# A new written order for the last two stages of a gated attention and feed-forward kernel

## The chip, the cores and the metric

The kernel runs on one core of a Trainium2 chip. The metric is the device time of one execution in microseconds (us), lower is better. A core has TensorE (PE in the rows; its weight loads are PEld), VectorE (DVE), ScalarE (ACT), GpSimd (POOL) and SyncE (SP), which here only issues DMAs. Each engine works through its own instructions in the order in which the program wrote them, and waits at an instruction until what it reads is ready and the buffer that it writes is free.

## The reference

The result is a gated mix of linear attention and a feed-forward layer over the same input, in float32: 2048 tokens, width 640, 32 heads of 20 features, hidden width 1728.

```python
g = _sigmoid((x * gate_w).sum(-1, keepdims=True))
qkv = ...                                     # x @ wqkv, by head
pq = jnp.einsum("bhsd,hdf->bhsf", q, w_phi)
phi_q = jnp.concatenate([_softmax(pq, axis=-1), _softmax(-pq, axis=-1)], axis=-1)
...                                           # phi_k the same from k
kv = jnp.einsum("bhsf,bhsd->bhfd", phi_k, v)
z  = jnp.einsum("bhsf->bhf", phi_k)
num = jnp.einsum("bhqf,bhfd->bhqd", phi_q, kv)
den = jnp.einsum("bhqf,bhf->bhq", phi_q, z)[..., None] + 1e-6
a = (num / den) @ wo                          # heads joined
b = silu(x @ w1) @ w2
out = g * a + (1 - g) * b
```

## The kernel before, in words

Nearly every product is made of three float32r matmuls: both factors are split into a high part (a cast on ACT) and a low part (a subtraction on DVE or POOL). The kernel first sums keys and values over all tokens, then runs the feed-forward layer in pairs of weight rows over two halves of the tokens, and ends with two stages whose order is written out by hand in two strings, `TAIL` and `FIN`. A loop pops the words of a string one by one and calls what stands under each word; `inorder` ties every instruction to the one before it on the same engine, so the string is the order of all five engines at once, SP's DMA issues included.

`TAIL` finishes the feed-forward layer and starts the queries: `fm`/`fs` join the query weights with the feature map (`pwq`), `qp12` to `qp15` are the query products of the last four token tiles (128 tokens each), `hm`/`hp` two last hidden rows, `im`/`ia` ten output products (`o`) and their additions, `km`/`kp` eleven small transposes that turn the key-value sums (`pkvt`).

`FIN` takes the other twelve token tiles and writes the result. A word has a letter and numbers:

- `q3p`: query product of the fourth of these tiles, 30 matmuls of 320 columns. Then on DVE `m`, `s0`, `s1` (extremes and differences), on ACT `e` (exponential), on POOL `z` and `M` (two 128x1280 products), on DVE `S`, `Z`, `P`, `i`, `k` (sums and factors), on ACT `g` (two copies and two DMAs that send the features to memory, `q_out`).
- `t05`, `f05`: transposes of features on PE for token blocks 0, 1 and 7 (256 tokens each) and their copy on ACT. The other blocks come back transposed by DMA (`j`).
- `n04`: product of features with key-value sums for block 0, head group 4 (`pn`, into PSUM); `h02` casts the pair of groups 4 and up into the high part of `oT` (ACT L1769), `l02` subtracts the low part (DVE L1774).
- `z0m`, `z0h`, `z0l`, `z0s`, `z0d`: the leftover columns of block 0. They are multiplied, split, stored to memory (`r_store`, L1798) and loaded into other partitions of `oT` (`r_place`, L1801, called the placing DMA below).
- `w02a`, `w02b`: the two halves of one output product of pass 0 (blocks 0 and 1), 15 matmuls `pa<-oT,wo` (L1836). Pass 1 is blocks 2 and 3, pass 2 blocks 4 and 5, passes 3 and 4 blocks 6 and 7. `y` loads the feed-forward part, `c` gates it (POOL), `d` adds it (DVE L1860), `o` stores the result.
- `x5l`, `x5s`: load and split of input columns for later query products.

A placing DMA writes partitions that the casts of the same block have written over, so it comes after all `h` and `l` of its block, and no `w` of a pass starts before both placing DMAs of its blocks have landed:

```python
def r_place(u):
    nc.sync.dma_start(
        o_cols(u)[KD : P - KD].rearrange("r c s w -> r (c s) w").bitcast(F32),
        r_d[u].rearrange("(r c) s w -> r (c s) w", c=NG),
    )
```

PSUM tiles of the last stage come from four banks named `single` and two pairs for query products, and a product waits until its bank has been read.

Of the kernel before, what the change touches and what calls it, by code (L numbers as in the profile page):

```python
# [73 lines left out]
Y43l v14 Y41h Y42l Y41l e14 xf r14 G43l m14 l14  # L74
"""
TAIL = """
fl1 xl0 hm012 hp012 fm1 fl2 fm2 ol4 fl5 fl4 fs1 fs2 fm4 fl3 fs4 wa fm0 fm5 fs0 fs5 fm3 W fs3 qp12
q012 q112 qp13 q013 qe12 os4 qn12 wb hm013 q113 qe13 xl2 qs13 xs2 hm113 hp013 qp14 ol2 q114 q014
hm112 qs12 qn13 qN13 xl1 os2 xs1 im0 qc13 ia0 qe14 hp113 qn14 qs14 im1 qc12 qP13 qi13 ol1 os1 ol3
qN12 ol0 km kp qN14 os0 qp15 q015 q115 qw13 hp112 ia1 is0 im2 ia2 qP12 is1 xs0 qi12 is2 qc14 qP14  # L80
qm13 os3 qw12 qm12 qe15 im3 ia3 im4 qn15 ia4 im5 qi14 qw14 qm14 is3 is4 qN15 ia5 ig5 im6 ia6 is5
qs15 ig6 im7 qc15 ia7 ig7 qP15 qi15 qw15 qm15 im8 ia8 im9 ia9 ig9 is7 ig8 is6
"""
PASS = """
h0a wh ka h1a h1b h0b us0 wl uh0 xh1 us1 uh1 ul0 h2a h2b us2 h3a ul1 xh3 uh2 h3b xh0 kb xh4 xl3 xh2
# [58 lines left out]
NSEV = (4, 5)  # L144
TPOSE = (0, 1, 7)
FIN = """
q0p t11 q0m q0s0 x10l t01 x4s x10s t00 t05 q1p x3s t12 f01 x14l t03 x14s q0s1 q0e q0z q0S f11 t15
f05 f00 q1m t13 q1s0 f12 x7l f15 z1m z0m n00 f03 z0h q1s1 y03 x5l z1h z1l x6l n01 t02 z0l q0Z t14
f13 t04 q1e q1z y01 f02 t10 x9l q0P z1s f14 n02 q0i q0k f10 n03 z0s h00 n10 n11 f04 q0M x8l x5s n12
n14 l00 n13 h10 q1S x7s q2p q1Z n04 h01 h12 q1P h11 q1i q0g q1k q1M x9s l11 h02 l10 l12 l01 l02 z0d  # L150
q1g x8s q2m z1d q2s0 q3p q2s1 q2e q3m q3s0 q3s1 q2S x12l q2z w00a w00b q3e w02a q2Z w02b q2P q2i q2k
q3S q3z j20 q3Z j21 x6s q3P j22 q4p x13l q3i q3k y02 d02 q2M q2g q5p w01a z2m q4m x11l q3M q4s0 x17l
n20 o02 q4s1 q5m q3g y00 d00 o00 x11s q4e q4z q5s0 y04 q5s1 n22 w01b z2h z2l n23 z2s n24 n21 w04a
q5e h20 h22 q4S j30 d01 q4Z q4P q4i q5z j32 q4k l20 h21 l21 w04b q4M q7p q5Z l22 n30 j31 n31 d04
x13s q5S q4g z3m z3h x15l q5P q5i q5k z3l q7m q5M q7s1 z3s z2d n34 n32 h32 h30 y14 x15s l32 o01 n33
x12s h31 q6p w03a q5g l30 l31 z3d q7s0 q6m w03b q6s1 q6s0 q7e q7S x16l q6e w14a q7z w10a q6z o04 j41
q7Z q7P q7i w10b q8p q7k q7M q6S w14b q7g q6Z q6P q6i q6k q6M q9p x17s q8m y11 q8s1 d14 q6g y10 q8s0
q8e j42 d10 q8z n44 d03 q9m j40 n42 z4m z4h z4l o14 q9s1 n40 n41 h40 n43 h42 h41 o10 w12a w12b o03
y12 w11a l40 q9s0 q8S w11b x16s q11p j50 j52 j51 q8Z q8P q8i q8k q9e q9z n54 d12 l42 z5m q9Z q9S z4s
q8M q8g n52 n53 z5h y23 d11 q9P q9i q9k n50 n51 q10p z5l y20 h50 w13a z5s h51 o11 l41 z4d w13b h52  # L160
o12 l50 l51 l52 z5d q11m gl q9M w20a w20b q11s1 y22 y13 q11s0 q10m w23a q9g q10s0 q11e q11z q11S j60
q10s1 q10e q10S w23b j62 w22a w22b j61 q10z d20 q11Z o20 q11P d23 w24a n60 n61 q11i q11k z6m q10Z
z6h d22 o22 n62 y24 n63 q10P h60 h61 n64 w24b w21a q10i q10k q10M q11M t73 d13 h62 z6l t71 l62 t72
f73 f71 t70 t74 f72 o23 z6s y21 t75 l60 w21b y30 c30 n72 l61 z6d d24 d21 n73 f75 z7m f70 n70 o13 f74
n74 z7h z7l n71 h70 o24 h71 w32a y34 c34 h72 l72 o21 w34a w34b w30a w30b l71 l70 z7s z7d w32b y42
y32 c42 d34 w40a w42a w42b o34 w40b w44a d30 o30 w44b y40 y44 c32 d32 o32 d42 o42 c40 d40 c44 o40
d44 o44
"""
ORDERS = (HEAD, O1, O2, O3, O4, O5, O6, O7, O8, O9, O10)
KEPT = (0, 2)  # L170
# [1813 lines left out]
```

## Time and profile before

| | |
|---|---|
| median of 3 runs | 700.91 us (700.59 to 701.91) |
| profiled execution, its own time | 701.84 us |
| span of its trace | 700.1 us |
| busy: PE, PEld, DVE, ACT, POOL | 99%, 84%, 66%, 45%, 58% |
| chain that ended last: PE, DMA, DVE, ACT | 95%, 2%, 1%, 1% |

The span runs from the first to the last instruction; 1.74 us of the execution lie outside it. In the trace `TAIL` begins at 478.3 us with its first product on PE, and `FIN` at 540.4 us. Times in the rows are counted from the start of the span.

### The profile page before, as it was taken

What the parts mean: (1) busy time and instruction counts of PE and PEld (TensorE: products, weight loads), DVE (VectorE), ACT (ScalarE), POOL (GpSimd) and SP (SyncE); (2) the same over time, 40 slices, a digit from 0 to 9 for tenths busy, and PEclk for the clock granted to TensorE, in tenths of its full rate; (3) what the DMA queues carried; (4) which work ended last, traced back from release to release, by engine and by line L of the source; (5) the groups of instructions that cost most, each with busy time, mean ns of one, the idle gap of its engine ahead of it and who ended that gap; (6) DMA issues with size and microseconds to landing.
All of it is one profiled execution on the core that took longest, in us unless ns stands there. A gap on an engine that the chain in (4) does not pass through costs nothing.

```text
span 700.1 us, 11997 instructions
## 1 busy us (share of the span) xinstructions
PE 691.8 (99%) x4530; PEld 586.8 (84%) x4530; DVE 464.6 (66%) x773; ACT 311.9 (45%) x556; POOL 407.7 (58%) x313
## 2 busy tenths in 40 slices
PE   9999999999999999999999999999999989999998
PEld 7888888888888888888888888788988878888878
DVE  4687978887434465677845556567695788878832
ACT  5344555446554433334455233425561755544230
POOL 2376876595672554574495555840499876665332
PEclk9999999999999999999999999999999999999999
DMA  8447888877584565489386444628013357998944
GB/s 308 144 171 277 323 292 301 284 275 240 172 284 157 204 217 173 155 303 340 115 303 218 138 156 126 202 82 265 25 62 130 122 148 216 227 244 210 215 142 133
DMA packets 88919, 141.75 MB, mean 202 GB/s; under 512 B 38498, under 2 KB 52086, under 8 KB 88862
## 3 DMA queue, kind: packets, MB, share of 16 engines
q1 hardware_dynamic: 83422, 133.77, 59.6%
q10 hardware_dynamic: 5440, 7.21, 2.9%
q8 instruction: 36, 0.59, 0.4%
q14 instruction: 21, 0.17, 0.1%
HBM read 88.61 MB, written 45.14 MB: 191 GB/s over the span
## 4 chain that ended last, share of the span: by engine, by line
PE 95%; DMA 2%; DVE 1%; ACT 1%; SPq 0%; issue 0%; DVEq 0%; ACTq 0%
PE kvp L622 18%; PE o L1240 12%; PE a L1110 10%; PE pa L1836 10%; PE o L1199 9%; PE pq L598 9%; PE o_m L1262 3%; PE ph L688 3%; PE b L1110 3%; PE c L1110 3%; PE d L1110 3%; PE pn L1758 2%; PE hp L707 2%; PE kvt L609 2%; DMA oT<-r_d 1%; PE kvp L493 1%
## 5 line engine op out<-in xcount | busy, mean ns | idle before, releaser
L1230 DVE TENSOR_TENSOR acc<-acc,o 128x512 f32<-128x512 f32 x118 | 77.3, 682 | 42.3 <-PE o L1240 35.0
L622 PE MATMUL kvp<-wh,xa 128*128 128x480 f32 (+2 forms) x420 | 90.3, 358 | 0.0
L622 PEld LDWEIGHTS kvp<-wh,xa 128*128 128x128 f32 x420 | 72.8, 188 | 10.0
L1836 PE MATMUL pa<-oT,wo 128*128 128x512 f32 (+1 forms) x375 | 72.3, 350 | 2.7 <-DMA oT<-r_d 2.7
L1836 PEld LDWEIGHTS pa<-oT,wo 128*128 128x128 f32 x375 | 59.4, 188 | 13.9 <-ACT eq L1337 2.4
L1199 PE MATMUL o<-u,w 128*128 128x512 f32 x280 | 65.5, 390 | 0.0
L1199 PEld LDWEIGHTS o<-u,w 128*128 128x128 f32 x280 | 52.4, 188 | 11.0
L1126 POOL TENSOR_TENSOR u<-v,u 128x512 fp32r<-128x512 f32 x18 | 23.3, 1296 | 65.3 <-ACT u L1125 65.3
L1354 POOL TENSOR_TENSOR ez<-eq,zbc 128x1280 f32<-128x1280 f32 x16 | 47.7, 2980 | 20.3 <-ACT eq L1337 20.0
L1094 POOL TENSOR_TENSOR v<-v,v 128x512 f32<-128x512 f32 x36 | 46.9, 1302 | 16.5 <-DVE u L1126 7.7
L650 POOL TENSOR_TENSOR ek<-ek,st 128x1280 f32<-128x1280 f32 x16 | 38.3, 2394 | 30.8 <-DVE st L649 18.9
L1124 ACT ACTIVATE v<-v 128x512 f32<-128x512 f32 x33 | 20.9, 632 | 78.2 <-DVE v L1143 35.2
L598 PE MATMUL pq<-wq,xb 128*128 128x320 f32 x360 | 55.1, 310 | 0.0
L598 PEld LDWEIGHTS pq<-wq,xb 128*128 128x128 f32 x360 | 53.3, 188 | 2.0 <-issue 1.5
L622 PE MATMUL kvp<-wl,xa 128*128 128x480 f32 (+2 forms) x210 | 47.6, 356 | 0.0
L1390 POOL TENSOR_TENSOR eq<-eq,sm 128x1280 f32<-128x1280 f32 x16 | 37.9, 2369 | 16.1 <-DVE sm L1384 15.8
L233 POOL TENSOR_TENSOR xa<-xra,xa 128x512 fp32r<-128x512 f32 (+1 forms) x26 | 28.4, 1113 | 24.1 <-ACT xa L231 23.2
L622 PEld LDWEIGHTS kvp<-wl,xa 128*128 128x128 f32 x210 | 36.6, 188 | 4.8
L1126 DVE TENSOR_TENSOR u<-v,u 128x512 fp32r<-128x512 f32 x24 | 18.5, 769 | 29.6 <-ACT u L1125 28.2
L1110 PE MATMUL a<-xo,wc 128*128 128x512 f32 x132 | 33.5, 389 | 0.0
L1400 ACT COPY ez<-eq 128x2400 uint16<-128x2400 uint16 x10 | 22.0, 2200 | 21.5 <-POOL eq L1390 21.5
L1273 POOL TENSOR_TENSOR acc<-acc,G 128x512 f32<-128x512 f32 x15 | 20.3, 1382 | 17.6 <-DVE acc L1204 17.6
(252 smaller groups left out, 1579.3 us busy)
## 6 DMA issues: line engine op xcount, KB each, us to landing
w<-w_d SPq DMA_DIRECT2D x20, 640.0 KB
sa<-s_d SPq DMA_DIRECT2D x18, 512.0 KB
w_d<-aw SPq DMA_DIRECT2D x14, 640.0 KB
xr<-xT SPq DMA_DIRECT2D x27, 256.0 KB
m_d<-ez ACTq DMA_DIRECT2D x10, 640.0 KB
ra<-w SPq DMA_DIRECT2D x18, 320.0 KB
wb<-w_d SPq DMA_DIRECT2D x9, 640.0 KB
w_k<-w SPq DMA_DIRECT2D x8, 640.0 KB
```

The lines of the kernel that those rows point to most:

```text
L598: nc.tensor.matmul(dst, xt[c][:, hx, :], w[:, c, hw, lo : lo + n], start=first, stop=(hx == 1 and c == NC - 1))
L622: nc.tensor.matmul(kv_cols(t, lo, hi), xt[c][:, hx, :], WKV[hw][:, c, w_cols(lo, hi)], start=(n == 0), stop=(n == 3 * NC - 1), skip_group_ ...
L650: return lambda: nc.gpsimd.tensor_tensor(groups(e), groups(e), spread(st[:, 1, :]), op=ALU.mult)
L1094: nc.gpsimd.tensor_tensor(v[i], v[a], v[b], op=ALU.subtract)
L1110: last["mm"] = nc.tensor.matmul(out, lhs, rhs, start=(first and i == 0), stop=(stop and i == len(todo) - 1), skip_group_check=True)
L1126: eng.tensor_tensor(u[:, 1, :], v, u[:, 0, :].bitcast(F32), op=ALU.subtract)
L1199: nc.tensor.matmul(o, lhs, rhs, start=(n == 0), stop=(n == len(todo) - 1))
L1230: nc.vector.tensor_tensor(acc[j][m], acc[j][m], o, op=ALU.add)
L1240: nc.tensor.matmul(o, ws[hw], x()[hx], start=(first and i == 0), stop=(i == len(PASSES) - 1), skip_group_check=True)
L1354: nc.gpsimd.tensor_tensor(ez, Q[t]["e"], zbc, op=ALU.mult)
L1390: nc.gpsimd.tensor_tensor(groups(q["e"]), groups(q["e"]), spread(q["sm"][:, 2 * H : 4 * H]), op=ALU.mult)
L1836: nc.tensor.matmul(pa[:, a, :], wo_tile[0][:, c, hw, ds], o[:, c, ho, :size], start=(i == 0), stop=(i == len(TERMS) - 1),)
```

## The change

Only the two strings differ: the same words in another order. No instruction, tile size or DMA is added or taken away. One line of each string:

```diff
 FIN = """
-q0p t11 q0m q0s0 x10l t01 x4s x10s t00 t05 q1p x3s t12 f01 x14l t03 x14s q0s1 q0e q0z q0S f11 t15
...
+q0p q0m q0s0 t05 x4s t00 f05 f00 t01 x10l x10s x3s q1p q0s1 t11 q0e x14l q0S q1m t12 q0z q1s0 x9l
...
 TAIL = """
-fl1 xl0 hm012 hp012 fm1 fl2 fm2 ol4 fl5 fl4 fs1 fs2 fm4 fl3 fs4 wa fm0 fm5 fs0 fs5 fm3 W fs3 qp12
...
+hm012 hp012 fl1 fm1 fs1 wa fl5 fl4 fm4 fl2 fs4 fm2 fs2 fm0 fm5 fl3 fm3 km W fs5 fs0 fs3 ol0 qp12
```

On PE, `TAIL` now has the transposes `km` right behind `fm3` instead of between `im1` and `qp15`, and `hm112` behind `qp15`. In `FIN`, `t11` goes behind `q1p`, `n04` before `q2p` instead of behind it, and the products of a pass swap places among themselves.

**ACT before the first output product.** Rows of the built program on ACT, from the last cast of block 0 (`oT<-pn_1`, `h01`, `h12`, `h11` above it) to the copies of `q1g` (L1400); `xb` is a split of later input. Before:

```order
L1769 CAST oT_5620<-pn_1_5634 128x2x256
L1400 COPY ez_5525<-eq_5439 128x20x120
L1404 COPY sm_5437<-eq_5439 128x256
L1405 DMA m_d_104<-ez_5525 256x1x1280
L1406 DMA m_d_104<-sm_5437 256x1x128
L231 CAST xb_0_5699<-xrb_0_5602 128x512
L1769 CAST oT_5620<-pn_2_5683 128x256
L1400 COPY ez_5592<-eq_5502 128x20x120
```

And of the change:

```order
L231 CAST xb_0_5648<-xrb_0_5524 128x512
L1769 CAST oT_5614<-pn_1_5631 128x2x256
L1769 CAST oT_5614<-pn_0_5609 128x2x256
L1400 COPY ez_5521<-eq_5439 128x20x120
L1404 COPY sm_5437<-eq_5439 128x256
L1405 DMA m_d_104<-ez_5521 256x1x1280
L1406 DMA m_d_104<-sm_5437 256x1x128
L231 CAST xb_2_5660<-xrb_2_5605 128x512
L1769 CAST oT_5614<-pn_2_5665 128x256
L1400 COPY ez_5568<-eq_5503 128x20x120
```

One input split (of 128x512) moved ahead of the copies of `q0g` and another came in its place; the cast of `pn_2`, which is `h02`, stays behind `q0g` and one split.

**DVE before pass 2.** The low parts of block 5 (`l5`, three rows L1774 into `oT`) and the first steps of query tile `q11` (L582 to L589); L1793 is `z5l`. Before:

```order
L1793 TENSOR_TENSOR rT_6452<-pr_6435,rT_6452 128x128
L1774 TENSOR_TENSOR oT_6333<-pn_1_6317,oT_6333 128x2x256
L1774 TENSOR_TENSOR oT_6333<-pn_0_6462,oT_6333 128x2x256
L1774 TENSOR_TENSOR oT_6333<-pn_1_6447,oT_6333 128x2x256
L1774 TENSOR_TENSOR oT_6333<-pn_2_6430,oT_6333 128x256
L582 TENSOR_REDUCE mmq_6413<-pq_6381 128x32
```

And of the change:

```order
L1793 TENSOR_TENSOR rT_6448<-pr_6419,rT_6448 128x128
L1384 SCALAR_TENSOR_TENSOR sm_6274<-pq_6243,g,sm_6274 128x64
L1860 TENSOR_TENSOR y_2_6330<-pa_2_6333,y_2_6330 128x512
L1774 TENSOR_TENSOR oT_6378<-pn_2_6460,oT_6378 128x256
L582 TENSOR_REDUCE mmq_6415<-pq_6383 128x32
L583 TENSOR_REDUCE mmq_6415<-pq_6383 128x32
L589 TENSOR_TENSOR eq_6416<-pq_6383,mmq_6415 128x32x20
L1774 TENSOR_TENSOR oT_6378<-pn_0_6436,oT_6378 128x2x256
L1774 TENSOR_TENSOR oT_6378<-pn_1_6439,oT_6378 128x2x256
```

Two of the three low parts of block 5 (`l50`, `l51`) moved behind three steps of `q11`.

**PE before pass 3.** The last transposes of block 7 (`pT`), its products (`pn`), and the output product `w21` (`pa_1`) of which half stood between them. Before:

```order
L1651 MATMUL pT_5_6720<-ident,eq_6500 128x128
L1651 MATMUL pT_5_6720<-ident,eq_6414 128x128
L1836 MATMUL pa_1_6667<-oT_6333,wo 128x512 x7
L1758 MATMUL pn_1_6734<-fT_1_6702,kvw 64x256 x2
L1758 MATMUL pn_1_6734<-fT_3_6700,kvw 64x256 x2
```

And of the change:

```order
L1651 MATMUL pT_4_6718<-ident,eq_6416 120x128 x2
L1651 MATMUL pT_0_6726<-ident,eq_6516 120x128 x2
L1651 MATMUL pT_0_6726<-ident,eq_6416 120x128 x2
L1758 MATMUL pn_1_6732<-fT_1_6707,kvw 64x256 x2
L1758 MATMUL pn_1_6732<-fT_3_6716,kvw 64x256 x2
```

The second half of `w21` moved ahead of all transposes, which the products now follow at once.

## Rows read from the trace of the kernel before

**Rows 1.** Page, busy time: us (share of the span) and instructions.

```profile
PE 691.8 (99%) x4530; PEld 586.8 (84%) x4530; DVE 464.6 (66%) x773; ACT 311.9 (45%) x556; POOL 407.7 (58%) x313
```

**Rows 2.** Two stretches: length, busy PE, PEld, DVE, ACT, POOL; clock, DMA share, GB/s.

```profile
560.00:580.00 20.00, 17.80 (x104) 15.73 (x103) 18.13 (x30) 9.98 (x13) 15.99 (x10) 1.00 0.62 157
...
600.00:620.00 20.00, 19.55 (x117) 16.42 (x116) 17.75 (x29) 9.51 (x13) 13.25 (x7) 1.00 0.83 226
```

**Rows 3.** TensorE's waits, 476 to 700 us: total, times, longest.

```profile
PE pa L1836 <- DMA oT<-r_d: 2.7, 2, 2.2
PE pT L1651 <- ACT fT L1665: 0.3, 1, 0.3
```

**Rows 4.** Chain that ended last, 515 to 571 us: start, length, what.

```profile
515.83 4.60 PE pq L598 x30
...
540.40 4.39 PE pq L598 x30
544.79 1.53 PE pT L1651 x14
...
564.32 0.61 PE pn L1758 x4
...
564.95 0.38 ACT oT L1769
...
566.64 4.82 DMA oT<-r_d
```

**Rows 5.** Timeline of ACT, 554 to 565 us: start, length, instruction, idle before.

```profile
554.10 1.28 ACT L1337 ACTIVATE eq<-eq 128x1280 f32<-128x1280 f32 x1
...
558.03 0.43 ACT L231 CAST xb<-xrb 128x256 fp32r<-128x256 f32 x1
...
560.71 2.21 ACT L1400 COPY ez<-eq 128x2400 uint16<-128x2400 uint16 x1
...
564.30 0.62 ACT L231 CAST xb<-xrb 128x512 fp32r<-128x512 f32 x1 [1.07 <-issue]
```

**Rows 6.** Timeline of POOL, 555 to 561 us.

```profile
558.32 2.36 POOL L1390 TENSOR_TENSOR eq<-eq,sm 128x1280 f32<-128x1280 f32 x1
```

**Rows 7.** Chain that ended last, 607 to 666 us.

```profile
607.73 5.15 DMA oT<-r_d
...
613.02 5.60 PE pa L1836 x23
...
650.21 15.58 PE pa L1836 x68
```

**Rows 8.** Timeline of DVE, 644 to 651 us.

```profile
644.18 0.29 DVE L1793 TENSOR_TENSOR rT<-pr,rT 128x128 fp32r<-128x128 f32 x1 [1.11 <-ACT rT L1788]
...
646.28 1.62 DVE L1774 TENSOR_TENSOR oT<-pn,oT 128x512 fp32r<-128x512 f32 x3 [1.21 <-ACT oT L1769]
647.82 0.81 DVE L582 TENSOR_REDUCE mmq<-pq 128x32 f32<-128x640 f32 x1
...
650.13 0.82 DVE L589 TENSOR_TENSOR eq<-pq,mmq 128x640 f32<-128x640 f32 x1
```

**Rows 9.** Timeline of SP, the placing DMA of block 5.

```profile
648.08 0.67 SPq L1801 DMA_DIRECT2D oT<-r_d  x1
```

**Rows 10.** Timeline of PE, 668 to 676 us.

```profile
668.29 3.72 PE L1836 MATMUL pa<-oT,wo 128*128 128x512 f32 x15
671.85 2.69 PE L1651 MATMUL pT<-ident,eq 128*120 128x128 f32 x22
674.29 1.87 PE L1836 MATMUL pa<-oT,wo 128*128 128x512 f32 x7
676.10 1.08 PE L1758 MATMUL pn<-fT,kvw 120*64 120x256 f32 x8
```

**Rows 11.** Timeline of SP, two loads of `y` before pass 3.

```profile
669.44 0.91 SPq L1823 DMA_DIRECT2D y<-fb_d  x2
```

**Rows 12.** Timeline of PE, the first nine matmuls of the kernel.

```profile
1.05 4.21 PE L463 MATMUL warm<-ones 128*128 128x512 f32 x9 [1.05 <-DVE ones L272]
```

More of the change, by code (lines that the diff above doesn't have):

```diff
@@ L76 @@
 TAIL = """
-fl1 xl0 hm012 hp012 fm1 fl2 fm2 ol4 fl5 fl4 fs1 fs2 fm4 fl3 fs4 wa fm0 fm5 fs0 fs5 fm3 W fs3 qp12
[L78 to L82, printed above, removed]
+hm012 hp012 fl1 fm1 fs1 wa fl5 fl4 fm4 fl2 fs4 fm2 fs2 fm0 fm5 fl3 fm3 km W fs5 fs0 fs3 ol0 qp12
+q012 xl2 q112 qp13 q013 xs2 xl0 q113 qe12 qs12 qe13 hm113 ol1 wb qn12 qN12 qc12 hm013 hp013 qn13
+qp14 ol4 kp os4 qN13 xl1 os0 os1 q114 qs13 im0 qc13 ia0 im1 ol3 qP12 qP13 qp15 q014 qe14 ol2 qi13
+qi12 hp113 q015 qw13 hm112 q115 qn14 ia1 im2 os2 qN14 is1 ia2 qw12 xs1 hp112 qm13 qe15 qn15 qs15
+qc15 im3 ia3 im4 qm12 xs0 ia4 os3 im5 qs14 qc14 is3 ia5 qN15 im6 ia6 ig5 is5 qP14 qP15 qi14 qw14 im7
+ia7 ig6 ig7 is4 im8 ia8 ig8 qi15 qm14 is0 is2 qw15 qm15 im9 ia9 is7 is6 ig9
 """
@@ L146 @@
 FIN = """
-q0p t11 q0m q0s0 x10l t01 x4s x10s t00 t05 q1p x3s t12 f01 x14l t03 x14s q0s1 q0e q0z q0S f11 t15
[L148 to L167, printed above, removed]
+q0p q0m q0s0 t05 x4s t00 f05 f00 t01 x10l x10s x3s q1p q0s1 t11 q0e x14l q0S q1m t12 q0z q1s0 x9l
@@ new lines @@
+f01 t03 t13 t15 x8l z0m f11 f12 f03 f15 x14s n00 z1m z0h f13 z1h q1s1 q1e q1z n01 t14 t02 t10 z0l
+x5l y01 f14 t04 z1l q0Z f10 q0P z0s x7l q0i n10 n11 h00 n14 f02 l00 q0k q0M n02 f04 q1S n03 h12 n12
+x5s h01 l12 q1Z q1P q1i q1k q1M n13 x9s l01 h11 h10 l10 l11 q0g x7s z1s n04 h02 q2p q1g x8s l02 q2m
+q2s1 q2s0 z0d q2e q2z z1d x11l x6l x6s q3p q3m q3s0 q3s1 q2S q3e q2Z q2P w02a q3z y03 q2i q2k x12l
+q2M j20 w02b q3S x11s q3Z q3P q3i q3k x17l q3M w00a w00b q4p y02 d02 j21 q5p j22 q2g q4m q4s1 z2m
@@ new lines @@
+q4s0 q3g q5m z2h x13l z2l q5s1 q5s0 n20 q4e o02 q4z z2s y00 d00 w01a q4S w01b d01 x15l n22 n24 n23
+q4Z q4P q4i y04 q5e q4k q5z q5Z n21 q5S h20 w04a w04b q4M x13s j30 h22 h21 j32 l21 q7p n30 z3m q5P
+q5i l22 q4g d04 j31 n34 q5k z3h o01 z3l z3s h32 q7m n31 q5M h30 l20 z2d q7s0 l30 o04 n32 x15s o00
+n33 q6p h31 l31 w03a l32 z3d q7s1 w03b w10a x12s q5g x17s y14 q7e q7z x16l y10 q6m q6s1 q6s0 q7S q6e
+w14a w10b w14b j41 q8p q7Z q7P q7i q7k q9p q6z y11 j42 q6S q6Z q7M z4m n44 n42 x16s q6P q6i n43 q6k
@@ new lines @@
+d10 j40 n40 q8m q7g o10 n41 q8s1 w11a y12 d03 w12a q8s0 d14 q9m o03 w12b q6M o14 q6g q8e z4h w11b
+q8z z4l q9s0 z4s j50 h40 h42 q9s1 q9e q11p j52 z5m l42 q9z j51 q8S q8Z q8P q8i q8k q8M q9Z n50 n52
+h41 d11 q8g z5h l40 q9S q9P y22 q9i l41 o11 n54 z5l z5s q9k n53 d12 h52 l52 q11m q11s0 h51 n51 h50
+l50 gl o12 q10p z4d l51 y13 z5d w13a q11s1 w13b y20 y23 w20a q10m q10s0 w20b q9M w22a q9g q10s1 w23a
+j60 w23b q10e q10S w22b d13 d20 w24a q10z q10Z j62 n64 z6m o13 q11e q11z j61 o20 q10P n62 q10i q10k
@@ L168 @@
+n63 q10M q11Z n60 q11S d23 o23 d22 q11P z6h q11i q11k n61 w24b w21a w21b y32 z6l q11M t71 y24 t75
+h60 h62 h61 t72 f71 f72 t73 l60 f73 t74 f75 f74 t70 l62 n72 n73 z7m f70 z6s l61 y21 d24 n74 z7h n70
+n71 d21 h70 o24 z6d o22 w30a w34a y30 c30 y34 c34 w30b z7l c32 l70 h72 w34b w32a w32b h71 l71 o21
+z7s l72 d30 z7d y42 w40a w42a w42b o30 c42 d34 o34 d32 y44 y40 c40 d42 c44 o32 w40b d40 o42 w44a o40
+w44b d44 o44
 """
```

## The prediction

> **What bounds the kernel now.** I read the page first: PE is busy for 691.8 us [rows 1], so work that is only reordered can give back 8.3 us at most, over the whole kernel. The wait table of the part that is reordered comes next. PE waits there twice for a placing DMA, 2.7 us together and 2.2 us the longer time, and once for a copy of transposed features, 0.3 us [rows 3]. The stretches show where: PE is busy 17.80 of 20 us from 560 to 580 and 19.55 of 20 from 600 to 620, with the clock at 1.00 in both [rows 2]. Little else can be gained but what PE loses when it changes between kinds of matmul, and the drain at the end, which has the same last instructions in both orders. So I ask of each wait whether the new order moves what ends last there.
>
> **First placing DMA, before pass 0.** The chain runs backwards from the first `pa`: a placing DMA lands 4.82 us after its issue at 566.64; ahead of that is `h02`, a cast of 0.38 us at 564.95 [rows 4]. `h02` needs `n04`, which ended at 564.93, so at first sight PE's late `n04` is at fault, and the change puts it one query product (4.39 us) earlier. But ACT tells more: it copies and sends `q0g` from 560.71, then splits an input tile at 564.30, and only then reaches `h02` [rows 5]. ACT would have come to `h02` at 564.9 whatever PE did. The new order on ACT keeps `h02` behind `q0g` and behind one split of the same size. And `q0g` starts when POOL's product `q0M` ends, at 558.32 + 2.36 = 560.68 [rows 6], which waits in turn for `q1z` and the exponential `q1e` at 554.10 [rows 5]. Is that earlier? PE reaches `q1p` sooner by the four transposes `t11` that go behind it, 4 x 1.53 / 14 = 0.44 us [rows 4]. On ACT, however, a 128x256 split (`x14s`, 0.43 us by the same shape [rows 5]) now stands ahead of `z0h` and `q1e`. The two cancel, so relative to the start of `FIN` I take 0 for the issue of the placing DMA, with 0.5 us either way. PE itself comes earlier, since `n04` no longer cuts the query products apart, and waits that much longer: the wait grows from 2.2 to some 2.6 us, and the gain of the cut is lost in it.
>
> The Trainium skill (DMA: Bandwidth & Descriptors, Anatomy of one DMA) gives a DMA, by a fit for the GpSimd path, some 2.0 us of fixed cost plus its bytes over 436 GB/s. By that an 80 KB placing DMA would land within 2.2 us and PE would not wait at all. The trace disagrees, with 4.82 and 5.15 us [rows 4, 7], and the sum goes by the trace; by the page it would end near 700.0 us.
>
> **What `TAIL` gives.** Between large products the transposes `km` cost more than themselves: the query product behind them takes 4.60 us where an undisturbed one takes 4.39 [rows 4], and PE loses about 0.1 us more on entering them. Behind `fm3`, itself a small matmul, that is saved. I take -0.3 us (bounds -0.5 and 0; zero if `hp013` or `q014` on DVE come late, whose banks the query products behind them need). The chain above hangs on the start of `FIN`, so this gain is kept.
>
> **Second placing DMA, before pass 1.** It is issued at 607.73 and lands 5.15 us later; `pa` begins at 613.02 [rows 7]. The new DVE order has `l20` between `q7m` and the low parts of block 3, one 128x512 subtraction more (0.65 us, since two and a half such in a row take 1.62 [rows 8]), against `z3m` standing one product earlier on PE (0.4 us) and a short low part put last. I take +0.1 us (-0.3 to +0.4). The wait of 0.5 us remains.
>
> **Third one, before pass 2, where nothing waits now.** The placing DMA of block 5 is issued at 648.08 [rows 9]. The run of 68 `pa` from 650.21 takes 15.58 us, 0.229 each, so pass 2 (behind the 15 matmuls of `w13`) begins at 650.21 + 15 x 0.229 = 653.65 [rows 7]. With a landing of 4.82 to 5.15 us the data is there at 652.90 to 653.23, 0.4 to 0.75 us ahead. In the change `l50` and `l51` stand behind three steps of `q11`. Those three take 650.13 - 647.82 = 2.31 us. From `z5l`, which ends at 644.47 as now, I count a factor (0.3), an addition (0.65), `l52` (0.4), the three steps (2.3) and two low parts at 1.62 x 2 / 2.5 = 1.3, together 649.4 [rows 8]. The issue moves by 1.3 us and the slack is gone: PE would wait 0.5 to 0.9 us. But the landings were read where PE waited; that pass 2 did not wait says only that this one took under 5.57 us. If it lands in 4 us nothing waits. I take +0.3 us, bounds 0 and 0.9.
>
> **Passes 3 and 4.** `w21` is no longer cut. Its second half took 676.10 - 674.29 = 1.81 us where 7 x 0.229 is 1.60, and the 15 matmuls ahead of the transposes 671.85 - 668.29 = 3.56 where 3.44 are due [rows 7, 10]. That is -0.3 us (bounds -0.35 and 0). The copies of the transposes (ACT) must then follow each other without a gap; they take about as long as the six transposes and the first product. A cost stands against it: `t73` needs the bank of `w21`, which `d21` frees after adding `y21`. That load is issued at some 669.4 as now [rows 11], but `d21` is wanted when `w21` ends, now at 671.85 + 1.60 = 673.5 [rows 10]. With the 4.82 us of the nearest landing the data comes at 674.2, and `d21` frees the bank 0.65 us later, at 674.9, where PE, two and a third transpose groups on, wants it at 674.5. I take +0.1 us (0 to 0.5).
>
> **The sum.** -0.3 + 0 + 0.1 + 0.3 - 0.3 + 0.1 = -0.1 us on the profiled execution's 701.84 us, thus 701.74. That execution lies 0.93 us above the median of the three runs; on the median the forecast is **700.8 us**. Two other cuts saved or kept elsewhere in `FIN` (the order of `z2m`, `n20`, `w01`) leave as many changes of matmul kind as before and count as nothing; the loads that are issued in another order land far ahead of their use. I take 0.2% of this time, 1.4 us, as what a measurement can tell from no change.
>
> **Rivals.**
>
> *The new order removes the first wait.* For it: `n04` is out of the way, and no more than a cast, a subtraction and an issue lie between it and the landing. PE will arrive about 0.35 us earlier, at 569.1, so it decides whether the last of these DMAs is issued before 569.1 - 4.82 = 564.3, 2.3 us sooner than now. Against it: ACT reaches `h02` only behind `q0g`. The price would be -2.2 and -0.35 on top of the sum: 698.2 us. Chance 0.15.
>
> *The placing DMA of block 5 is the new bound.* The mechanism is pass 2 above, with one thing more: the load of `y13`, 256 KB, is now issued just ahead of it and behind it before. At 226 GB/s, the rate of the second stretch [rows 2], that is 1.2 us. Issued at 649.4 and landed 5.15 + 1.2 us later, it holds PE until 655.75, a wait of 2.1 us instead of 0.3, and the time is 702.6 us. It decides from a landing of about 6 us on. Against it: pass 2 did not wait before, with other DMAs in flight. Chance 0.08.
>
> *The clock falls in the longer first wait.* In the idle 2.2 us of before the granted clock stayed at 1.00 [rows 2], its upper level of 2.4 GHz. The wait is longer in the change, and if the clock went to 1.2 GHz, pass 0 would run slowly: the first nine matmuls of 512 columns took 4.21 us, about 0.45 each [rows 12], against 0.229. If it lasted as long as in those rows, it would cost half of 4.2 us: 702.9 us. Chance 0.03. The Trainium skill (TensorE: Matmul & The Clock Gate, Part 1) says that an idle array falls back to the half rate; here the trace agrees only for the start, not for a wait of 2.2 us.
>
> *Small sums off on either side.* Gains that all come to their better bound give -1.1 us, costs that all come to their worse one +1.9. I leave 0.02 for each side beyond 1.4 us.
>
> **How the numbers follow.** The forecast has 0.70; its own range is 699.5 to 702.2. Faster by over 0.2%: 0.15 + 0.02 = 0.17. Slower: 0.08 + 0.03 + 0.02 = 0.13. The range of 8 in 10 reaches from 698.8 to 702.4, which leaves out most of the first rival's cases and the two slow ones.
>
> **What would show it.** In the chain of the changed kernel, ACT's `q0g` copy and `h02` still stand ahead of the first placing DMA, and PE waits over 2.2 us for it. The idle time before pass 1 is 0.4 to 0.9 us. A new row of PE waiting for `oT<-r_d` near 653 shows the third term; the seven `pa` between transposes and products are gone. I am wrong if PE does not wait before pass 0, if `FIN` begins later than before, or if DVE, whose order moved most, makes query products wait for a bank.

## The result

The change is slower. Four executions take 704.25 us in the median (704.04 to 706.18) where the kernel before takes 700.75; the ratio is 1.0044, 95% interval 1.0029 to 1.0058. The forecast of 700.8 us and its range, up to 702.4, are both missed. The profiled execution took 704.36 us, 2.52 more than the profiled one of before, and its span is 702.6 us, 2.5 more. The medians differ by 3.5 us, 1.0 more than the two traced executions, of which that of before was 1.1 us above its kernel's median; what follows accounts for the 2.5 us between the traces.

The page gives busy times that answer to [rows 1]:

```profile
PE 692.3 (99%) x4530; PEld 587.7 (84%) x4530; DVE 464.2 (66%) x773; ACT 311.7 (44%) x556; POOL 407.2 (58%) x313
```

The share of PE has not moved, which tells nothing. TensorE's waits from 476 us on (total, times, longest) tell more:

```profile
PE pa L1836 <- DVE pq L1341: 2.4, 1, 2.4
PE pa L1836 <- DMA oT<-r_d: 2.2, 1, 2.2
PE pT L1651 <- ACT fT L1665: 0.3, 1, 0.3
```

In [rows 3] there were two waits for a placing DMA, 2.7 us together. The wait of 0.5 us before pass 1 has gone, the first one still lasts 2.2 us, and a new one of 2.4 us is put down to DVE. The stretches (length, busy PE, PEld, DVE, ACT, POOL; clock, DMA share, GB/s) place it:

```profile
560.00:580.00 20.00, 17.84 (x105) 16.35 (x104) 16.84 (x27) 9.90 (x13) 15.17 (x10) 1.00 0.77 174
...
640.00:660.00 20.00, 17.56 (x96) 14.27 (x96) 12.23 (x21) 7.25 (x10) 8.16 (x3) 0.91 0.89 246
652.00:654.50 2.50, 0.07 (x1) 0.02 (x1) 1.49 (x2) 2.13 (x2) 1.45 (x1) 1.00 0.66 216
654.50:656.00 1.50, 1.49 (x4) 1.22 (x5) 0.59 (x2) 0.00 (x0) 1.50 (x2) 0.50 0.94 148
656.00:658.00 2.00, 2.00 (x7) 1.59 (x6) 0.00 (x0) 0.00 (x0) 2.00 (x1) 0.53 1.23 254
658.00:660.00 2.00, 2.00 (x10) 1.64 (x9) 0.17 (x1) 0.00 (x0) 0.84 (x1) 1.00 1.03 253
```

The same stretch of before was full, at full clock:

```profile
640.00:660.00 20.00, 20.00 (x119) 16.92 (x118) 16.17 (x24) 9.05 (x10) 8.29 (x3) 1.00 0.83 212
```

From 652 to 654.5 us PE does next to nothing, and when it starts again its granted clock is 0.50 for some 3.5 us: only 11 matmuls run from 654.5 to 658, where 15 are due at 0.229 us each. So two things happened before pass 2, a wait and behind it a fall of the clock. Timeline of PE in the change (start, length, instruction, idle before):

```profile
481.39 7.16 PE L350 MATMUL pwq<-constb,wTq 120*128 120x120 f32 x60
...
539.92 4.56 PE L598 MATMUL pq<-wq,xb 128*128 128x320 f32 x30
...
648.45 3.61 PE L1836 MATMUL pa<-oT,wo 128*128 128x512 f32 x15
654.51 11.81 PE L1836 MATMUL pa<-oT,wo 128*128 128x512 f32 x43 [2.44 <-DVE pq L1341]
```

and of before:

```profile
481.71 7.16 PE L350 MATMUL pwq<-constb,wTq 120*128 120x120 f32 x60
...
540.24 4.56 PE L598 MATMUL pq<-wq,xb 128*128 128x320 f32 x30
...
650.05 9.33 PE L1836 MATMUL pa<-oT,wo 128*128 128x512 f32 x40
```

With them the 2.5 us can be laid out. The change was 0.32 us ahead before its first new word (481.39 against 481.71), which is chance. From the start of `FIN` to `w13` it needs 108.53 us instead of 109.81, a gain of 1.28. Pass 2 was due 15 x 0.229 = 3.44 us after that, at 651.89, and began at 654.51: a loss of 2.62. The 43 matmuls behind take 11.81 - 0.17 (the modelled end, 3.61 - 3.44) where 43 x 0.229 = 9.85 are due: 1.79 lost to the clock. The rest, -0.3, is passes 3 and 4: from the first `pn` behind pass 2 to the end the change needs 34.00 us (668.58 to 702.58) and the kernel before 34.35 (665.71 to 700.06). Together -0.3 - 1.3 + 2.6 + 1.8 - 0.3 = +2.5.

Three more rows are from the chain that ended last (start, length, what): the first query products, the first placing DMA, which lands after 4.5 us, and the matmuls ahead of and into pass 1, in which nothing waits any more.

```profile
489.35 9.00 PE pq L598 x60
...
566.21 4.51 DMA oT<-r_d
...
608.33 10.32 PE pa L1836 x45
```

What did pass 2 wait for? DVE's `L1341` is a sum of query tile 10, which no output product reads. The matmuls need the two placing DMAs of blocks 4 and 5. The timeline of SP has that of block 5 at 647.50, behind a load of `y` (256 KB, `y13`), and that of ACT has the features of `q9` (640 and 64 KB) sent at the same moment:

```profile
645.93 0.47 SPq L1823 DMA_DIRECT2D y<-fb_d  x1
647.50 0.69 SPq L1801 DMA_DIRECT2D oT<-r_d  x1
...
647.41 0.54 ACTq L1405 DMA_DIRECT2D m_d<-ez  x1
648.04 0.58 ACTq L1406 DMA_DIRECT2D m_d<-sm  x1
```

In the kernel before, by the timeline of ACT, this store began 1.05 us behind the placing DMA (issued at 648.08, [rows 9]):

```profile
649.13 0.54 ACTq L1405 DMA_DIRECT2D m_d<-ez  x1
```

From the issue at 647.50 to the first matmul at 654.51 are 7.0 us. The trace also holds the semaphore that tells of each landing, which no view lists: this DMA's was last raised at 654.26, 6.77 us after the issue and 0.25 us ahead of that matmul. So PE waited for the DMA, and DVE's sum only ended at the same moment. In the kernel before, the DMA of block 5 landed at 652.89 by its semaphore, after 4.82 us. The experiments ask whether the neighbours did that, and whether the fall of the clock belongs to the wait.

### The profile page after: what moved, and what is told of

It is laid out like the page before. It is cut to its first block, busy times and chain, and to the rows that moved or that the text cites. A ratio compares the mean times of both kernels' runs of the same rounds, so it can differ in the third digit from the quotient of the medians.

```text
span 702.6 us, 11988 instructions
## 1 busy us (share of the span) xinstructions
PE 692.3 (99%) x4530; PEld 587.7 (84%) x4530; DVE 464.2 (66%) x773; ACT 311.7 (44%) x556; POOL 407.2 (58%) x313
## 4 chain that ended last, share of the span: by engine, by line
PE 94%; DMA 2%; ACT 2%; issue 1%; SPq 0%; DVE 0%; POOL 0%; ACTq 0%; DVEq 0%; POOLq 0%
PE kvp L622 18%; PE o L1240 12%; PE pa L1836 10%; PE a L1110 10%; PE o L1199 9%; PE pq L598 8%; PE o_m L1262 3%; PE ph L688 3%; PE b L1110 3%; PE c L1110 3%; PE d L1110 3%; PE pn L1758 2%; PE hp L707 2%; PE kvt L609 2%; PE kvp L493 1%; PE kvq L493 1%
## 5 line engine op out<-in xcount | busy, mean ns | idle before, releaser
L1400 ACT COPY ez<-eq 128x2400 uint16<-128x2400 uint16 x10 | 22.0, 2197 | 20.7 <-POOL eq L1390 20.7
```

## The experiments

Each execution's mean clock is listed, so that a fall can be counted without a trace: 1.00 means none, 0.998 or 0.997 mostly one, 0.995 two (in f6 0.994 is one longer fall, by its trace). The diffs show only the words around a move, not whole lines of the string. Of the 105 executions of the kernel before that ran beside the experiments, 44 are at 1.00 (medians 700.5 to 701.0 us by chip) and nearly all others at 0.997 or 0.998 (medians 701.9 to 702.4).

| kernel | median us | ratio to before | at clock 1.00 |
|---|---|---|---|
| f0_change_again | 703.96 | 1.0036 (1.0021 to 1.0050) | 0 of 10 |
| e1_low_parts | 701.18 | 0.9992 (0.9974 to 1.0010) | 4 of 10 |
| e2_load_behind | 701.63 | 1.0000 (0.9985 to 1.0016) | 5 of 10 |
| e3_features_behind | 701.34 | 0.9996 (0.9980 to 1.0012) | 5 of 8 |
| e4_both | 700.05 | 0.9984 (0.9967 to 1.0001) | 5 of 10 |
| e5_both_again | 700.06 | 0.9978 (0.9965 to 0.9991) | 5 of 9 |
| f2_cast_first | 701.19 | 1.0003 (0.9991 to 1.0014) | 3 of 10 |
| f3_low_parts_first | 701.76 | 1.0011 (0.9992 to 1.0030) | 2 of 10 |
| f5_stores_behind | 702.00 | 1.0007 (0.9991 to 1.0023) | 5 of 12 |
| f6_product_first | 704.14 | 1.0038 (1.0025 to 1.0050) | 0 of 12 |
| f7_exp_first | 698.86 | 0.9959 (0.9945 to 0.9974) | 5 of 6 (the sixth 0.999) |
| t1_tail_alone | 701.60, once | | 1.00 |
| b2_load_ahead | 707.65, once | | 0.995 |

Two executions of e3_features_behind, at 979 and 3147 us, stand apart for a reason not known and are not counted.

**e1_low_parts: the low parts back in front.**

```diff
-h52 l52 q11m q11s0 h51 n51 h50 l50 gl o12 q10p z4d l51 y13 z5d w13a
+h52 l52 h51 n51 h50 l50 l51 q11m q11s0 gl o12 q10p z4d y13 z5d w13a
```

> The change, with the low parts l50 and l51 ahead of q11m and q11s0 again; the load of y13 still goes ahead of the placing DMA of block 5. That DMA is then issued about 1.0 us earlier (646.5 instead of 647.5), ahead of the feature store of q9 (647.4) instead of beside it. Theory 'the load': it is y13 that lengthens the landing to 6.8 us, so it lands at about 653.2 and PE waits some 1.2 us before pass 2; about 701.2 us if the clock holds, 703 if it falls again. Theory 'the store': the 704 KB of q9's features lengthen it; ahead of them it lands after about 5 us, PE does not wait, the clock stays, about 700.0 us.

701.18 us. In the traced execution the clock fell behind the first wait instead, as two stretches of the trace show:

```profile
560.00:580.00 20.00, 17.81 (x95) 15.88 (x94) 16.77 (x27) 9.85 (x13) 15.11 (x10) 0.91 0.77 181
572.00:574.00 2.00, 2.00 (x6) 1.58 (x6) 2.00 (x2) 0.45 (x1) 0.84 (x1) 0.53 0.96 293
```

In the timeline PE runs into pass 2 almost without a stop:

```profile
650.02 10.34 PE L1835 MATMUL pa<-oT,wo 128*128 128x512 f32 x43
```

The 43 matmuls take 0.3 us more than their due (43 x 0.229, and 0.17 for the modelled end): the DMA landed at 653.58 by its semaphore, 5.40 us after its issue, and was wanted at 650.02 + 3.44 = 653.46. So an issue 0.8 us ahead of the store (648.17 against 648.97 on the timelines of SP and ACT) is nearly enough, with the load still in front; the 6.8 us of the load theory did not come. That the clock had fallen before moves everything in this trace by some 1.6 us.

**e2_load_behind: only the load of `y13` moved.**

```diff
-z4d l51 y13 z5d w13a
+z4d l51 z5d y13 w13a
```

> The change, with the load of y13 issued behind the placing DMA of block 5 instead of ahead of it; the low parts stay late, so the DMA is issued at 647.5 as in the change, beside the feature store of q9. Theory 'the load': the landing shrinks by the 1.2 us that 256 KB take, to about 5.5 us, PE waits 1.0 us and the clock stays up: about 701.0 us. Theory 'the store': the landing stays near 6.8 us, the wait near 2.4 us, the clock falls: about 704.2 us.

701.63 us, and as the load theory said. In the timeline of SP the issue of the two placing DMAs ends at 647.53; the second began 0.68 us before that, at 646.85. It landed at 652.29 by its semaphore, after 5.44 us. In the timeline of PE pass 2 starts 0.14 us later, after a wait of 1.0 that is put down to an exponential on ACT, and in this execution the clock stays at 1.00:

```profile
644.55 2.98 SPq L1801 DMA_DIRECT2D oT<-r_d  x2
...
647.82 3.61 PE L1836 MATMUL pa<-oT,wo 128*128 128x512 f32 x15
652.43 7.81 PE L1836 MATMUL pa<-oT,wo 128*128 128x512 f32 x33 [1.00 <-ACT eq L1337]
```

**e3_features_behind: only the store of `q9` moved.** Its two DMAs get a word of their own.

```diff
-j60 w23b q10e q10S
+w23b q10e q9o j60 q10S
```

> The change, with only the two DMAs of the feature store of q9 moved behind the exponential of q10 on ACT (from 647.4 to about 653.0), and the transposing load j60 that reads them behind that. The load of y13 and the low parts stay as in the change. Theory 'the load': nothing changes before pass 2, 704.2 us. Theory 'the store': the placing DMA of block 5 lands within about 5.2 us, the wait is 0.6 us or less and the clock stays: about 700.6 us, if block 6, whose transposed features then come 3 us later, is not late.

701.34 us, and as the store theory said, with the load still in front. The chain has a landing of 4.7 us:

```profile
647.70 4.69 DMA oT<-r_d
```

and the timeline of PE a wait of 0.25 us:

```profile
652.53 7.81 PE L1846 MATMUL pa<-oT,wo 128*128 128x512 f32 x33 [0.25 <-DMA oT<-r_d]
```

The move has its own price: the transposed features of block 6 come late, and the table of waits has a new one for them.

```profile
PE pn L1768 <- DMA fT<-m_d: 0.8, 1, 0.8
```

The landings are 6.8 us with the load ahead and the store beside it, 5.4 with the store and the load behind, 4.7 with the load ahead and no store near. So the load ahead adds 1.3 us where the store goes out beside the DMA; without the store it adds nothing that shows, since 4.7 is no more than the 4.82 of before. The Trainium skill (DMA: Bandwidth & Descriptors, Queues, rings and completion order) says that SP's and ACT's queues are served by the same 16 engines in turn, each queue in its own order; these three runs agree with it in that the store on ACT's queue lengthens the landing of a DMA on SP's (6.8 us against 4.7).

"Beside" has a side, however. Before pass 1 of the change, a store of 640 KB starts 0.12 us behind the placing DMA of block 3 (timelines of SP, ACT and PE), where before pass 2 it started 0.09 us ahead:

```profile
606.99 0.69 SPq L1801 DMA_DIRECT2D oT<-r_d  x1
...
607.11 0.54 ACTq L1405 DMA_DIRECT2D m_d<-ez  x1
...
608.17 10.48 PE L1836 MATMUL pa<-oT,wo 128*128 128x512 f32 x45
```

That DMA landed in 3.90 us by its semaphore (610.88), and PE goes into pass 1 without a wait. A store that starts a moment behind the DMA did not hold it up; why the order of two issues counts for so much is not shown.

**e4_both and e5_both_again: low parts and load put right together.** `z5d` then goes right behind `z4d`.

> The change, with l50 and l51 ahead of q11m and q11s0 and with y13 behind the placing DMA of block 5, which is then issued right behind that of block 4, at about 645.9. By both theories it lands before 652.0, PE does not wait before pass 2 and the clock does not fall: 704.25 - 2.4 (wait) - 1.7 (slow matmuls) = about 700.1 us. If the clock falls near 655 for another reason than the wait, the slow matmuls stay: about 701.8 us.

> e4_both once more, to narrow its interval (0.9967 to 1.0001 before). If the two edits of pass 2 repair the change and the 1.6 us of lead that it has by pass 2 is kept, 1.2 to 1.5 us less than the kernel before, a ratio of 0.998; a mean clock of 1.00 in about half of the executions, as in the kernel before, since the wait of 2.2 to 2.4 us before pass 0 is still there.

700.05 and 700.06 us; by the narrower interval at most 0.9991 of the kernel before. PE runs through into pass 2 (timelines of SP and PE in e4_both):

```profile
645.14 1.59 SPq L1800 DMA_DIRECT2D oT<-r_d  x2
...
648.41 11.85 PE L1835 MATMUL pa<-oT,wo 128*128 128x512 f32 x51
```

The loss of the change is all in this one place: with these words moved, the lead that it had gathered by pass 2 is kept.

**b2_load_ahead: the kernel before with the load of `y13` in front.**

```diff
-l50 l51 l52 z5d q11m gl q9M w20a w20b q11s1 y22 y13 q11s0
+l50 l51 l52 y13 z5d q11m gl q9M w20a w20b q11s1 y22 q11s0
```

> The kernel before, with nothing changed but the load of y13, which goes ahead of the placing DMA of block 5 instead of 3.2 us behind it. Theory 'the load adds its 1.2 us': issued at 648.6 instead of 648.1, it lands at about 654.6 (648.6 + 4.8 + 1.2) where PE wants it at 653.5: a new wait of about 1 us before pass 2 and no other. Rival 'only the store counts': it lands at 653.4, no wait.

A wait of 2.83 us, more than either theory gave, and two falls of the clock. The load went out 1.2 us after the issue ahead of it, and the placing DMA behind it on the same queue only at 650.34, where the store of `q9` began at 650.27 (timelines of SP, ACT and PE):

```profile
649.83 0.33 SPq L1823 DMA_DIRECT2D y<-fb_d  x1
650.34 0.67 SPq L1801 DMA_DIRECT2D oT<-r_d  x1
...
650.27 0.55 ACTq L1405 DMA_DIRECT2D m_d<-ez  x1
...
657.63 6.65 PE L1836 MATMUL pa<-oT,wo 128*128 128x512 f32 x21 [2.83 <-DMA oT<-r_d]
```

In this trace all times up to here stand 1.1 us later than in that of before, since the clock fell behind the first wait; the rest of the delay is the load's. The chain gives the landing:

```profile
650.34 7.16 DMA oT<-r_d
```

These 7.2 us are of the size of the change's 6.8. The low parts ended at 649.04, so the load held the issue back by about 1.1 us, past the start of the store. One moved load makes a loss of the same kind in the old order too, in the one execution that there is.

**f0_change_again: how often does the clock fall?** The change itself.

> The change itself, once more, on a chip on which the kernel before is timed beside it: what counts is the mean clock of each execution. Theory 'each long wait may cost the clock': the wait before pass 0 (2.2 us) and that before pass 2 (2.4 us) each end with the clock at half for some 3.5 us in a part of the executions, so that fewer executions than of the kernel before (14 of 31) keep a mean clock of 1.00, and some show two falls (0.995). Those at 1.00 are then only 0.5 to 1.0 us over those of before at 1.00 (2.4 us of wait less a lead of 1.6), the others 1.7 us more for each fall: a median of 702.5 to 704. Theory 'the wait before pass 2 always costs it': none at 1.00, median 703 to 704.

703.96 us; no execution at 1.00, three at 0.995, as the second theory had it. Here the table of waits does name the DMA:

```profile
PE pa L1836 <- DMA oT<-r_d: 5.1, 2, 2.9
```

The chain has its landing at 7.25 us:

```profile
648.67 7.25 DMA oT<-r_d
```

And the stretches show that the clock fell behind both waits:

```profile
560.00:580.00 20.00, 17.78 (x94) 15.83 (x93) 16.76 (x28) 9.40 (x12) 15.08 (x9) 0.91 0.72 188
...
640.00:660.00 20.00, 17.08 (x98) 14.01 (x98) 13.19 (x22) 8.42 (x10) 8.14 (x3) 0.93 0.88 231
```

With the four of the result, none of 14 executions of the change kept its clock; two of them were traced.

**t1_tail_alone: the new `TAIL` with the old `FIN`.**

> The kernel before with the TAIL of the change alone. If the prediction's term is right, FIN's first product begins about 0.3 us earlier on PE (540.1 instead of 540.4) and the rest is as before: 0.3 us less in the span at the same mean clock. Rival: nothing is gained, 540.4.

Nothing is gained up to `FIN`. From the small products `pwq` to the start of `FIN` PE needs 539.23 - 480.70 = 58.53 us here, 58.53 in the change and 58.53 before (the two timelines above):

```profile
480.70 7.16 PE L350 MATMUL pwq<-constb,wTq 120*128 120x120 f32 x60
...
539.23 4.55 PE L598 MATMUL pq<-wq,xb 128*128 128x320 f32 x30
```

Behind that the old `FIN` has two waits of PE which neither the kernel before nor the change has, 0.6 us for POOL and 0.3 us for DVE, by the table of waits.

**f2_cast_first and f3_low_parts_first: the first wait.** Both stand on e4_both and put the last cast of block 0 ahead of the copies of `q0g`; f3, which the diff shows, also puts the low parts ahead of `q1P`.

```diff
-q1Z q1P q1i q1k q1M n13 x9s l01 h11 h10 l10 l11 q0g x7s z1s n04 h02 q2p q1g x8s l02 q2m q2s1 q2s0 z0d q2e q2z z1d
+q1Z n13 h11 h10 l01 l11 l10 z1s z1d n04 h02 l02 z0d q1P q1i q1k q1M x9s q0g x7s q2p q1g x8s q2m q2s1 q2s0 q2e q2z
```

> As e4_both, and before pass 0 the product n04 and the cast h02 stand ahead of the copies of q0g on ACT, the low parts of block 1 ahead of those of block 0 on DVE (still behind q1k), and both placing DMAs directly behind their low parts. They are then issued at 563.1 and 564.0 instead of 565.1 and 565.8. Theory 'issue': with the 4.5 us of the change they land at 568.5, PE does not wait before pass 0, the clock is 1.00 in all executions: 700.05 - 2.4 - 0.8 (half of the executions had lost 1.6) = about 697. Theory 'the store': the features of q0 (704 KB, sent at 563.0) go out beside them and the landing takes 6.8 us: lands at 570.8, the wait stays 2 us, about 700.

> As f2_cast_first, with the low parts of blocks 0 and 1 also ahead of q1P, q1i and q1k on DVE: the placing DMAs are issued at about 562.3 and 563.0, the first ahead of the store of q0, the second beside it; q1M, q1g and what follows them come 2 us later. Theory 'issue': no wait before pass 0, about 697 us, clock 1.00 in all executions. Theory 'the store': the second lands after up to 6.8 us, at 569.8, a wait of 1.1 us, 698.5. If what was pushed back on DVE holds PE later (q2, q3 or block 2), a new wait shows and the time is up to 2 us more.

In f2 the last placing DMA goes out at 562.99, 3.2 us earlier than in the change, and lands at 570.31, only 0.4 us earlier: the store of `q0` (561.97) is ahead of it, and loads and the store of `q1` follow. No load stands ahead of it (chain):

```profile
562.99 7.32 DMA oT<-r_d
```

In f3 they go out at 561.89 and 562.77, the second 0.2 us ahead of that store, and land in 4.08 and 4.36 us by their semaphores; pass 0 starts at 568.20 with no wait. But then the fifth query product waits 2.07 us for its bank, which DVE frees late (timeline of PE):

```profile
568.20 7.05 PE L1833 MATMUL pa<-oT,wo 128*128 128x512 f32 x30
577.32 10.56 PE L595 MATMUL pq<-wq,xb 128*128 128x320 f32 x60 [2.07 <-DVE sm L1381]
```

**f5_stores_behind and f6_product_first: the stores moved back.** On f2's order, both stores go behind the exponential of `q2`; f6, which the diff shows, also puts the product `q2z` ahead of the split `x8s` on POOL.

```diff
-q2p q1g x8s q2m q2s1 q2s0 q2e q2z x11l
+q2p q1g q2m q2s1 q2s0 q2e q2z x8s q0o q1o x11l
```

> As f2_cast_first, with the two feature stores that go out beside the placing DMAs of blocks 0 and 1 (of q0 and q1, 704 KB each, four DMA issues on ACT) moved behind the exponential of q2 on ACT. The placing DMAs are issued at 562.1 and 562.9 as there. Theory 'the store': the landing shrinks from 7.3 us to about 5, to 567.9, PE reaches pass 0 at 567.7 and waits no more than 0.5 us; the exponential of q2 comes 2 us earlier, so q4 does not wait for its bank as it did in f3_low_parts_first (2.1 us). No wait over 1 us is left, so most executions keep the clock at 1.00: 700.05 - 2.2 - 0.8 = about 697.5 us. Rival 'the issue of many DMAs at once': the landing stays 7 us whatever the stores do, wait 2 us, 700 to 701 us.

> As f5_stores_behind, with the POOL product of q2 ahead of the split x8, and that split ahead of the two feature stores on ACT, so that the product starts at 568.4 instead of 572.3. Theory 'the long wait may cost the clock': the wait of q4 for its bank (3.0 us) goes or shrinks under 1 us, no long wait is left in the two stages, nearly all executions have a mean clock of 1.00, and the time is 697 to 698 us where e4_both gave 700.06. Rival 'the clock falls there whatever PE does, in half of the executions': half of them stay at 0.998 or below, some 1.6 us above the others. Third case: the next query product waits in its place (q5 for the bank of q3), the wait has only moved on, and the time stays near 700.

No wait for a placing DMA in either (by the semaphores they land in 4.4 to 4.6 us), so the store theory holds here too; but the fifth query product waits 2.99 us in f5 (timeline of PE),

```profile
578.41 9.04 PE L595 MATMUL pq<-wq,xb 128*128 128x320 f32 x60 [2.99 <-DVE sm L1381]
```

and 3.73 in f6. In f5 ACT issues its four DMAs from 567.13 to 570.80 and only then comes to the split of `x8`, behind which POOL's product `q2z` stands (572.33). In f6 the product is ahead of the split, but it writes the buffer from which the store of `q0` reads. That store goes out at 567.60 and takes 5.04 us by the chain, and POOL stands idle for 6.67 us until it has ended (timelines of POOL and PE):

```profile
572.77 2.94 POOL L1351 TENSOR_TENSOR ez<-eq,zbc 128x1280 f32<-128x1280 f32 x1 [6.67 <-DMA m_d<-ez]
...
578.82 11.63 PE L595 MATMUL pq<-wq,xb 128*128 128x320 f32 x60 [3.73 <-DVE sm L1381]
```

So none of the three cases of f6's expectation came: the wait of `q4` neither went nor moved on to `q5`, it grew. Behind it the 60 matmuls take 11.63 us instead of the 9.04 of the trace of f5, whose clock stayed up, and no execution of f6 kept its clock.

**f7_exp_first: no long wait.** f3 with `q2e` and `q2z` ahead of `q1g`.

```diff
-q2p q1g x8s q2m q2s1 q2s0 q2e q2z x11l
+q2p q2m q2s1 q2s0 q2e q2z q1g x8s x11l
```

> As f3_low_parts_first (placing DMAs of blocks 0 and 1 at 561.9 and 562.6, ahead of the store of q0, no wait for them), with the exponential of q2 on ACT and its product on POOL ahead of the copies and the store of q1. The exponential starts at 567.2 instead of 569.9, the product at 568.4, into the buffer that the store of q0 has left by then; q4's bank is free at 574.4, before PE wants it (575.3). The store of q1 lands at about 575, then the product of q3 may start, and q5 waits about 1.4 us for its bank. Theory 'the long wait may cost the clock': with 1.4 us as the longest wait, most executions keep a mean clock of 1.00, and the time is 697 to 698.5 us. Rival 'the clock falls there in half of the executions whatever PE does': half at 0.998 or below. Third case: the buffer of q0 is free later than 568.4, a wait of 2 us or more comes back at q4, and the time is 700 or above.

698.86 us, 0.9959 of the kernel before (0.9945 to 0.9974) and the fastest of all. From 476 us on the longest wait is 0.5 us, and no execution is under 0.999, on a chip on which eight of eleven executions of the kernel before are at 0.998. Its waits of PE:

```profile
PE pq L595 <- DVE sm L1381: 1.0, 2, 0.5
PE pT L1648 <- ACT fT L1662: 0.3, 1, 0.3
```

## Why the prediction was wrong

**The step that failed is the third placing DMA, before pass 2** (+0.3 us, bounds 0 and 0.9). Its first half was right: the DVE order came as read, the low parts behind three steps of `q11`, and the slack was used up. The term was mis-sized in the landing, 6.8 us (7.25 in f0) in place of 4.82 to 5.15, and so it measured 2.6 us in place of 0.3. For the old neighbours the 4.82 us were right, to the hundredth. The rival on this DMA had the mechanism and the point from which it decides ("about 6 us"), and 1.2 us for the load; e2 gave back 1.4. What it left out is the store on ACT. Counted back from the start of `w13`, the store hardly moved: 0.92 us ahead of it before, 1.04 now. The placing DMA moved from 1.97 us ahead to 0.95, so the later low parts took its whole lead of 1.05 us over the store. The rows of before could have shown it: the prediction itself puts the issue at 649.4, and the store of before went out at 649.13. Two engines' orders met on the transfers, and I had costed each engine alone. The chance of 0.08 rested on "pass 2 did not wait before, with other DMAs in flight"; but the store of `q9`, the largest, had gone out 1.05 us behind it, and that was not looked at.

**The price of a wait was wrong too.** The forecast counts a wait at its length. Here 2.4 us of wait cost 2.4 and another 1.8 in slow matmuls. The rival on the clock saw this for the first wait at a chance of 0.03, because the clock had stayed at 1.00 in the one trace. It does fall there in some executions: the traces of e1, e5, f0 and b2 show it behind a first wait of 2.16 to 2.31 us (granted clock 0.91 from 560 to 580 us in each). In over half of its executions the kernel before, which has no other long wait, loses some clock; one trace could not show that. The Trainium skill (TensorE: Matmul & The Clock Gate, Part 1) says that an idle array falls back to half rate, and, of the change to the full rate, that its moment varies from run to run; these four traces agree with the first, and I had read the page against the single trace.

**The other terms.** `TAIL`: 0.0 in place of -0.3; the loss of 0.2 us behind `km` only moved to other query products (9.00 us for 60 matmuls where 2 x 4.39 are due; before, 4.60 for 30 [rows 4]). First placing DMA: the wait stayed, as forecast, at 2.2 instead of 2.6, since it landed in 4.5. Second one: its wait of 0.5 is gone, where +0.1 was forecast. This DMA went out no earlier, counted from the start of pass 0 (36.1 us behind it, 36.0 before), but landed in 3.90 us in place of 5.15, so the same step failed here too, the other way. Up to pass 2 `FIN` gained 1.3 us, of which I had none: 0.5 up to pass 0, 0.6 up to pass 1 with the wait, and 0.2 behind. Passes 3 and 4: -0.3 measured, -0.2 forecast, but only 0.14 of it came ahead of pass 3, where `w21` was joined. Without the 2.6 and 1.8 us of pass 2 the change would be 1.6 us faster than before (1.3 and 0.3); e4_both and e5_both_again have medians 1.45 and 1.62 us under those of the kernel before beside them. The 700.0 us that the prediction gives for a landing of 2.2 us does not come out of its terms: without its waits of 2.6, 0.6 and 0.3 us and the 0.1 for `d21` the sum would be near 697.2.

**The rival on the first wait** had -2.2 us as its price. f3, f5 and f6 show that most of it is not to be had in that way: PE comes earlier to a bank that the chain of `q2` over ACT, POOL and DVE frees no sooner. f7, which shortens that chain too, gets most of it: the span of its trace is 696.3 us, that of e4_both 698.1, both with the clock at 1.00.

## What to carry to other kernels

A DMA on which TensorE is about to wait is costed with its neighbours: what is issued ahead of it on its own queue, and what large transfer starts on another engine's queue at that moment. The landing of the trace before holds only for the neighbours of before, so look at every queue's issues in the two microseconds around it, and let the small DMA go out ahead of the large one: here 0.1 to 0.2 us ahead was enough, and 0.1 us behind was not. When a wait is removed, ask which buffer or bank the waiting engine reaches next, and follow its chain before counting the gain. And count the executions' clocks beside their times: a wait of 2 us and more may cost nearly as much again.

## What the hardware showed unexpectedly

The 15 traces hold 120 placing DMAs of 80 KB. By the semaphores of their landing 115 took 3.4 to 5.8 us and five took 6.8 to 7.3 (7.32 in f2). In these five, and in e2 (5.44), the 640 KB of a store had started on ACT's queue 0.07 to 1.0 us ahead; none of the other 114 had such a start in the 2.5 us ahead of it. With the store 0.12 to 0.13 us behind instead, before pass 1 in twelve traces, the landing took 3.7 to 4.0 us.

PE has 17 waits of 2 us or more in these traces, of 2.07 to 3.73 us. Behind ten of them the granted clock fell to its lower level (1.2 GHz); from 10 us on it fell nowhere else until the last few microseconds of the kernel. The shortest wait with a fall is 2.07 us (f3), the longest without one 2.99 (f5), and of the ten first waits of 2.16 to 2.44 us four had a fall. So the length of the wait alone does not decide it. A fall cost 1.8 us in the change and 2.6 in f6. f7 is the check: with no wait over 0.55 us from 10 us on in its trace, its six executions kept a mean clock of 0.999 or 1.00. What else decides stays open.
